# GEMM1 of blocks 3 to 8 of the first layer as seven products over two blocks, with streamed w_out and the second layer's w_in prepared beside it

## The chip, the cores and the metric

The kernel runs on one core of a Trainium2 chip. The metric is the device time of one execution in microseconds (us). Times of single instructions and stretches are read from a trace that the hardware profiler took of one execution. The engines are named as in the profile: PE (TensorE matmul), PEld (its weight loads), DVE (VectorE), ACT (ScalarE), POOL (GpSimd) and SP (SyncE, which issues the DMAs).

## The reference

```python
scores = scale * np.matmul(q_c, k_c.transpose(0, 1, 2, 4, 3))   # chunks of 64 positions
attn = np.exp(scores - np.max(scores, axis=-1, keepdims=True))
attn = attn / (np.sum(attn, axis=-1, keepdims=True) + 1e-09)
out = np.matmul(attn, v_c)
x = out.transpose(0, 2, 1, 3).reshape(4608, 512)
h = x @ w_in;  x = (h * np.cos(h)) @ w_out                       # first layer, w_in 512 x 2048
h = x @ w_in2; y = (h * (1 / (1 + np.exp(-1.702 * h)))) @ w_out2  # second layer
```

All is float32, with 8 x 8 heads, 576 positions and heads of 64.

## The kernel before

The 4608 tokens are nine blocks of 512 (j = 0 to 8), the hidden width 2048 is 16 slices of 128 (f = 0 to 15). Attention runs in 18 pairs of units (two units of 128 tokens), two pairs to a block. A float32 product is three matmuls of a split into a high and a low part (high x high, high x low, low x high), so GEMM1 of one slice and block is 12 matmuls of 128x512, and so is GEMM2.

A plain block has 16 steps. A step is `gemm1` of slice f (into `h`), the cosine chain of the slice on ACT and DVE in turns (ACT L484, DVE L487, ACT L493, ACT L496, DVE L499, then ACT L512 and DVE L515 for the high part `gh` and the low part `gl`), and `gemm2` of slice f - 2 (`LAG`). The first layer's blocks are all plain. While block j runs, attention of block j + 1 is done in it: scores and softmax of its two pairs at steps 0 and 7 (`SJ`), transposes 3 steps and values 5 steps later (`OFFSJ`).

The second layer does block 0 plainly and blocks 1 to 8 in four doubles of two blocks. `pair_of_slices` replaces GEMM1 of two slices on two blocks by seven products of half the depth (42 matmuls where the plain form has 48). The products need left factors (sums and differences of w_in, stored in DRAM as `wc` and loaded for each pair of slices by `load_factors` into `w_xh` and `w_xl`) and right factors (sums and differences of the activations, `right_factor`, kept in the buffers of w_in). The products accumulate in three PSUM tiles, `pb`, `pu` and `pc`. `copied` (L734) copies one to SBUF on ACT, `plus` (L738) adds `pu` to it on DVE, and the next product that accumulates on `pu` must wait until `plus` has read it:

```python
product(0, A11, u, True, False)
c11 = plus(c11)
...
run(6)
product(3, A_S2, u, False, False)
```

`run` puts GEMM2 matmuls of the first of the two blocks between the products (6, 10 and 8). The second block's activations are parked in SBUF. In the second half of a double its 16 GEMM2 steps of 12 matmuls run from the park, split just ahead by `split_park`, and right factors of the next double are made beside them.

The second layer's weights are loaded and converted (L204 to L247, `split_w_parts`) during block 8 of the first layer and block 0 of the second, where the left factors are made and stored as well.

The order on PE is written by hand. On the other engines the framework's scheduler sets it, and each engine then runs its instructions in that order.

Of the kernel before, what the change touches and what calls it, by code (L numbers as in the profile page):

```python
# [19 lines left out]
P = 128  # L20
# [92 lines left out]
def tile_chunk_attention_two_moe(  # L113
# [28 lines left out]
    S0, SJ = (2, 9), (0, 7)  # L142
    OFFS0, OFFSJ = (4, 6), (3, 5)
# [28 lines left out]
    wc = [dr.tile([2, P, 7, 2 * P], F32R, name=f"wc_{i}") for i in range(NP)]  # L172
# [8 lines left out]
    def load_w(dram, layer, which, f):  # L181

        t = wp.tile([P, DM, 2], U32, tag=f"{which}{f}", name=f"raw_{which}{f}")
        nc.sync.dma_start(out=t, in_=dram[f].bitcast(U32).rearrange("p (d w) -> p d w", w=2))
        raw[layer, which, f] = t

    def split_w(layer, which, f):
        for fn in split_w_parts(layer, which, f, layer == 1):
            fn()
        if layer == 1 and which == "i" and f % 2:  # L190
            left_factors(f // 2, T.pop(f - 1), T.pop(f))
# [3 lines left out]
    def split_w_parts(layer, which, f, by_dma=False):  # L195
# [34 lines left out]
        def p5():  # L230
            w = wp.tile([P, 2 * DM], F32R, tag=f"{which}{f}", name=f"{which}{f}")
# [29 lines left out]
    def load_pair(p):  # L261

        if 2 * p >= NU:
            return
        for u in (2 * p, 2 * p + 1):
# [3 lines left out]
        for u in (2 * p, 2 * p + 1):  # L269
# [154 lines left out]

    def att_values(p, tags=("a", "a")):
        for w in range(2):
            att_values_w(p, w, tags)
        for i in range(2):
# [5 lines left out]
    def load_x1(j):  # L434
        if j >= NB:
            return
        for k0 in range(0, KD, 2):
            t = qkp.tile([P, 2, N], F32, tag="qk", name="x1")
            nc.sync.dma_start(out=t, in_=y1[j][k0:k0 + 2].rearrange("k p n -> p k n"))
            xr[j, k0] = t  # L440

# [156 lines left out]
    for j in range(NB - 1):  # L598
        for i in range(PB):
            p = (j + 1) * PB + i  # L600
            s0, offs = (S0[i], OFFS0) if j == 0 else (SJ[i], OFFSJ)
            at((0, j, s0), att_scores, p)
            at((0, j, s0), att_softmax, p)
            at((0, j, s0 + offs[0]), att_transpose, p)
            at((0, j, s0 + offs[1]), att_values, p)
            at((0, j, s0 + offs[1]), load_pair, p + PB)
    at((0, NB - 1, 2), load_x1, 0)
    for k in range(KD):
        at((0, NB - 1, 4 + 2 * k), split_x1, 0, k)
# [8 lines left out]

    A11, A12, A_S1, A_S2, A_S3, A_S4, A22 = range(7)
    PRODUCTS = ("b11", "b21", "t1", "t2", "t3", "b22", "t4")  # L620

    def left_factors(i, t1, t2):
# [5 lines left out]
        for o, x, y, op in (  # L628
            (u[:, :H2], t2[:, :H2], t2[:, H2:], add),
            (u[:, H2:], u[:, :H2], t1[:, :H2], sub),  # L630
            (w[:, :H2], t1[:, :H2], t2[:, :H2], sub),
            (w[:, H2:], t1[:, H2:], u[:, H2:], sub),
        ):
            nc.vector.tensor_tensor(out=o, in0=x, in1=y, op=op)
        hi = ap.tile([P, 2 * DM], F32R, tag="a", name="s_hi")
        lo = ap.tile([P, 2 * DM], F32R, tag="a", name="s_lo")
        for k, src in ((0, u), (1, w)):
            c = slice(k * DM, (k + 1) * DM)
            split(hi[:, c], lo[:, c], src)
        for part, sums in ((0, hi), (1, lo)):  # L640
            first, second = (W[1, "i", 2 * i + k][part] for k in range(2))
            for ops, src in (((0, 2), first), ((2, 6), sums), ((6, 7), second[:, H2:])):
                nc.sync.dma_start(
                    out=wc[i][part, :, ops[0]:ops[1], :].rearrange("p o c -> p (o c)").bitcast(F32),
                    in_=src.bitcast(F32),
                )
# [13 lines left out]
    def right_factor(s, m, k):  # L660

        name = PRODUCTS[m]
        ja, jb = 2 * s + 1, 2 * s + 2
        b11, b12 = xr[jb, 0][:, k], xr[ja, 0][:, k]
        b21, b22 = xr[jb, 2][:, k], xr[ja, 2][:, k]
# [394 lines left out]
```

## Time and profile before

| | us |
|---|---|
| median of 3 runs | 1641.44 (1640.91 to 1643.64) |
| profiled execution, its own time | 1642.49 |
| span of the profiled execution | 1640.7 |
| PE busy | 1604.3 (98%) |
| DVE busy | 879.1 (54%) |
| ACT busy | 844.7 (51%) |

The span runs from the first to the last instruction on the core; 1.8 us of the execution's time lie outside it. The busy shares are means over stages that differ.

### The profile page before, as it was taken

To read this page: it belongs to the slowest core of one execution; us is meant where nothing else is said; L and a number is where in the kernel's file an instruction comes from. 1 tells how busy PE (TensorE), PEld (TensorE's weight loads), DVE (VectorE), ACT (ScalarE), POOL (GpSimd) and SP (SyncE) were. 2 spreads that over 40 slices of the span, in tenths; PEclk is the share of its full clock that TensorE was granted. 3 is DMA by queue.
4 is the path that set the end of the run, shared out by engine and by line. 5 is a ranking of instruction groups with operands and counts; after the bars stand their busy time and mean duration, and the time that the engine had idled before them with its cause. 6 is when DMAs were issued, how large, how long until landed. Compare 5 with 4: busy or idle time off the path is not lost.

```text
span 1640.7 us, 22795 instructions
## 1 busy us (share of the span) xinstructions
PE 1604.3 (98%) x9168; PEld 1321.0 (81%) x9168; DVE 879.1 (54%) x1427; ACT 844.7 (51%) x1419; POOL 57.0 (3%) x69
## 2 busy tenths in 40 slices
PE   5899999999999999999999999999999999999998
PEld 4678888888888888888888788888888888888887
DVE  7796445354445445454688884345434543454442
ACT  6796555455555545555677663343334333333331
POOL 1220000000000000000011110000000000000000
PEclk9899999999999999999999999999999999999999
DMA  9953111011111101110399764340424042404210
GB/s 357 329 117 90 40 44 60 14 66 39 52 40 65 39 16 63 40 52 27 122 282 337 215 186 153 123 163 24 161 115 167 19 170 106 173 14 154 99 68 27
DMA packets 60156, 181.59 MB, mean 111 GB/s; under 512 B 6417, under 2 KB 8465, under 8 KB 60049
## 3 DMA queue, kind: packets, MB, share of 16 engines
q1 hardware_dynamic: 50976, 163.60, 27.4%
q0 software_dynamic: 9072, 16.52, 5.7%
q8 instruction: 72, 1.18, 0.3%
q14 instruction: 36, 0.29, 0.1%
HBM read 130.02 MB, written 33.55 MB: 100 GB/s over the span
## 4 chain that ended last, share of the span: by engine, by line
PE 90%; DVE 3%; DMA 3%; issue 2%; ACT 1%; SPq 0%; POOL 0%; POOLq 0%; ACTq 0%; DVEq 0%
PE y L558 45%; PE h L460 23%; PE pu L723 11%; PE pc L723 5%; PE pb L723 3%; PE x L402 1%; DMA raw_i<-w_in 1%; PE s L295 1%; DMA i<-wt 1%; PE pt_ps L376 1%; DVE wt L218 1%; DMA y<-yo 1%; DVE wt L224 1%; DVE wt L207 0%; ACT wt L204 0%
## 5 line engine op out<-in xcount | busy, mean ns | idle before, releaser
L460 PE MATMUL h<-xh,i 128*128 128x512 f32 x1280 | 426.9, 395 | 15.1 <-DVE r L499 10.5
L558 PE MATMUL y<-o,gh 128*128 128x512 f32 x1152 | 299.8, 389 | 0.6 <-ACT gh L512 0.6
L460 PEld LDWEIGHTS h<-xh,i 128*128 128x128 f32 x1280 | 243.8, 190 | 69.2 <-DVE r L499 12.6
L558 PE MATMUL y<-gh,o 128*128 128x512 f32 x1152 | 295.4, 395 | 0.0
L558 PEld LDWEIGHTS y<-o,gh 128*128 128x128 f32 x1152 | 216.6, 188 | 46.1 <-ACT gh L512 1.0
L460 PE MATMUL h<-xl,i 128*128 128x512 f32 x640 | 252.3, 394 | 0.3 <-DVE xl L423 0.3
L558 PEld LDWEIGHTS y<-gh,o 128*128 128x128 f32 x1152 | 213.1, 188 | 44.6
L487 DVE SCALAR_TENSOR_TENSOR r<-h,r 128x512 f32<-128x512 f32 x144 | 99.4, 690 | 180.3 <-ACT r L484 180.2
L484 ACT ACTIVATE r<-h 128x512 int32<-128x512 f32 x144 | 85.7, 595 | 199.2 <-PE h L460 193.6
L499 DVE SCALAR_TENSOR_TENSOR r<-r,h 128x512 f32<-128x512 f32 x144 | 98.7, 685 | 117.4 <-ACT r L496 117.3
L558 PE MATMUL y<-o,gl 128*128 128x512 f32 x576 | 158.3, 389 | 0.0
L558 PE MATMUL y<-gl,o 128*128 128x512 f32 x576 | 158.3, 389 | 0.0
L460 PEld LDWEIGHTS h<-xl,i 128*128 128x128 f32 x640 | 122.1, 191 | 26.3 <-DVE xl L423 1.0
L515 DVE TENSOR_TENSOR gl<-r,gh 128x512 fp32r<-128x512 f32 x160 | 110.1, 688 | 55.7 <-ACT gh L512 54.9
L512 ACT ACTIVATE gh<-r 128x512 fp32r<-128x512 f32 x160 | 100.5, 628 | 69.5 <-DVE r L499 66.5
L738 DVE TENSOR_TENSOR part<-pu,part 128x512 f32<-128x512 f32 x96 | 66.2, 690 | 129.3 <-ACT part L734 89.2
L558 PEld LDWEIGHTS y<-gl,o 128*128 128x128 f32 x576 | 108.1, 188 | 22.5
L558 PEld LDWEIGHTS y<-o,gl 128*128 128x128 f32 x576 | 108.1, 188 | 22.5
L493 ACT ACTIVATE r<-r 128x512 f32<-128x512 f32 x144 | 91.1, 633 | 60.1 <-DVE r L487 59.8
L734 ACT ACTIVATE part<-pc 128x512 f32<-128x512 f32 x64 | 38.3, 599 | 162.5 <-PE pc L723 162.5
L723 PE MATMUL pu<-x_t,w_xh 128*128 128x512 f32 x384 | 118.2, 389 | 0.0
L700 ACT ACTIVATE r<-part 128x512 f32<-128x512 f32 x96 | 60.4, 629 | 64.7 <-DVE part L738 64.7
(92 smaller groups left out, 1843.9 us busy)
## 6 DMA issues: line engine op xcount, KB each, us to landing
w_xl<-wc SPq DMA_DIRECT2D x32, 896.0 KB, 6.4
w_xh<-wc SPq DMA_DIRECT2D x32, 896.0 KB, 4.6
qk<-qk SPq DMA_DIRECT2D x36, 512.0 KB, 4.4
raw_i<-w_in SPq DMA_DIRECT2D x32, 512.0 KB, 9.2
raw_o<-w_out SPq DMA_DIRECT2D x32, 512.0 KB, 9.2
v<-v SPq DMA_DIRECT2D x36, 256.0 KB, 3.5
y<-yo SPq DMA_DIRECT2D x36, 256.0 KB, 2.3
x<-y SPq DMA_DIRECT2D x18, 512.0 KB, 5.8
```

The costliest lines, as they stand in the source:

```text
L460: nc.tensor.matmul(out=h, lhsT=a[:, w0], rhs=b[:, k, :], start=(k == 0 and i == 0), stop=(k == KD - 1 and i == 2),)
L484: nc.scalar.activation(out=c["r"].bitcast(I32), in_=c["h"], func=AF.Copy, scale=INV_2PI)
L487: nc.vector.scalar_tensor_tensor(out=c["r"], in0=c["h"], scalar=INV_2PI, in1=c["r"].bitcast(I32), op0=ALU.mult, op1=ALU.subtract,)
L493: nc.scalar.activation(out=c["r"], in_=c["r"], func=AF.Sin, scale=math.pi)
L499: nc.vector.scalar_tensor_tensor(out=c["r"], in0=c["r"], scalar=-0.5, in1=c["h"], op0=ALU.add, op1=ALU.mult)
L512: nc.scalar.activation(out=c["gh"], in_=c["r"], func=AF.Copy)
L515: nc.vector.tensor_tensor(out=c["gl"], in0=c["r"], in1=c["gh"].bitcast(F32), op=ALU.subtract)
L558: nc.tensor.matmul(out=ys[d0], lhsT=a, rhs=b, start=(f == 0 and i == 0), stop=(f == NF - 1 and i == 2),)
L700: nc.scalar.activation(out=r, in_=h, func=AF.Sigmoid, scale=1.702)
L723: nc.tensor.matmul(out=out, lhsT=x, rhs=y, start=(start and k == 0 and n == 0), stop=(stop and k == 1 and n == 2), skip_group_check=True,)
L734: nc.scalar.activation(out=t, in_=src, func=AF.Copy)
L738: nc.vector.tensor_tensor(out=t, in0=u, in1=t, op=ALU.add)
```

## The change

Blocks 0 to 2 of the first layer stay plain. Blocks 3 to 8 become three doubles with the same seven products (`by_1024` now serves both layers). For this:

- the first layer's left factors are made in blocks 1 and 2 from the split weights (`left_factors0`) and stored to `wc`; a factor tile has eight parts where it had seven, 1 MB a half where it was 896 KB;
- w_out of the first layer is stored to DRAM in block 1 and streamed back slice by slice (`load_wo`, four buffers), since its buffers now hold the parked activations, the staged attention output and the second layer's new weights;
- attention of blocks 3 and 4 (four pairs) is done in block 2 (`SJ2`), that of blocks 5 to 8 in the second halves of the first two doubles (`SJ3`, four pairs in 11 steps). Its output is staged to SBUF in float32 and turned into right factors (`RIGHT_A`, `RIGHT_B`);
- the second layer's w_in is loaded, converted and made into left factors in the first halves of the three doubles (`prepare1` with stages 0, 1 and 2 in successive pairs of slices, at the slots `PREP`). The third double's second half loads it back (`load_w1`), and w_out of the second layer is converted there and in block 0 of the second layer.

```diff
-    S0, SJ = (2, 9), (0, 7)
-    OFFS0, OFFSJ = (4, 6), (3, 5)
+    S0, OFFS0 = (2, 9), (4, 6)
+    SJ1 = ((0, 3, 5), (7, 10, 12))
+    SJ2 = ((0, 3, 4), (1, 5, 6), (7, 10, 11), (8, 12, 13))
+    SJ3 = ((0, 3, 4), (1, 5, 6), (4, 7, 8), (5, 9, 10))
+    SR = (8, 10)
+    PREP = (0, 3, 5, 8, 11, 13, 16, 19)
...
+    J0 = 3
...
+                    nc.scalar.activation(
+                        out=XS[0, j](2 * b + i)[:, o * P:(o + 2) * P],
+                        in_=xs_t[p][i][:, b].rearrange("p w n -> p (w n)"),
+                        func=AF.Copy,
+                    )
+            return
...
+    for j, p0, starts in ((1, 2 * PB, SJ1), (2, 3 * PB, SJ2)):
+        for p, stages in enumerate(starts, p0):
+            for fn, f in zip((att_begin, att_transpose, att_end), stages):
+                at((0, j, f), fn, p)
...
+    def left_factors0(i):
+        parts = [W[0, "i", 2 * i + k] for k in range(2)]
+        t = []
+        for hi, lo in parts:
+            x = tp.tile([P, DM], F32, tag="t", name="w32")
+            nc.vector.tensor_tensor(out=x, in0=hi.bitcast(F32), in1=lo.bitcast(F32), op=ALU.add)
+            t.append(x)
+        left_factors(0, i, t, parts)
...
+    def store_wo(f):
+        hi, lo = W[0, "o", f]
+        for part, src in ((0, hi), (1, lo)):
+            nc.sync.dma_start(
+                out=wo[f][:, part * DM:(part + 1) * DM].bitcast(F32), in_=src.bitcast(F32)
+            )
+    def load_wo(f):
+        t = wp.tile([P, 2 * DM], F32R, tag=f"o{NF - 4 + f % 4}", name="wo")
+        nc.sync.dma_start(out=t.bitcast(F32), in_=wo[f].bitcast(F32))
+        W[0, "o", f] = t[:, :DM], t[:, DM:]
...
+    def prepare1(i, stage):
+        fs = (2 * i, 2 * i + 1)
+        for k, f in enumerate(fs):
+            if stage == 0:
+                load_w(w2_in, 1, "i", f, tag=f"o{k}")
+            elif stage == 1:
+                for fn in split_w_parts(1, "i", f, False, tag=f"o{2 + k}"):
+                    fn()
+        if stage == 2:
+            left_factors(1, i, [T.pop(f) for f in fs], [W[1, "i", f] for f in fs])
...
-    def load_factors(i):
+    def load_factors(layer, i):
         parts = []
         for part, tag in ((0, "xh"), (1, "xl")):
-            t = xp.tile([P, 7, 2 * P], F32R, tag=tag, name=f"w_{tag}")
-            nc.sync.dma_start(out=t.bitcast(F32), in_=wc[i][part].bitcast(F32))
+            t = xp.tile([P, 8, 2 * P], F32R, tag=tag, name=f"w_{tag}")
+            nc.sync.dma_start(out=t.bitcast(F32), in_=wc[layer][i][part].bitcast(F32))
...
+    RIGHT_A = [(5, k) for k in range(2)]
+    RIGHT_B = [(m, k) for k in range(2) for m in (1, 0, 2, 3, 6, 4)]
...
+    def act_second(layer, j, f, h, keep=None):
         r = tp.tile([P, N], F32, tag="t", name="r")
-        nc.scalar.activation(out=r, in_=h, func=AF.Sigmoid, scale=1.702)
-        nc.vector.tensor_tensor(out=r if keep is None else keep, in0=h, in1=r, op=ALU.mult)
+        dest = r if keep is None else keep
+        if layer == 0:
+            n = r.bitcast(I32)
+            nc.scalar.activation(out=n, in_=h, func=AF.Copy, scale=INV_2PI)
+            nc.vector.scalar_tensor_tensor(
+                out=r, in0=h, scalar=INV_2PI, in1=n, op0=ALU.mult, op1=ALU.subtract
+            )
+            nc.scalar.activation(out=r, in_=r, func=AF.Sin, scale=math.pi)
+            nc.scalar.activation(out=r, in_=r, func=AF.Square)
+            nc.vector.scalar_tensor_tensor(
+                out=dest, in0=r, scalar=-0.5, in1=h, op0=ALU.add, op1=ALU.mult
+            )
+        else:
+            nc.scalar.activation(out=r, in_=h, func=AF.Sigmoid, scale=1.702)
+            nc.vector.tensor_tensor(out=dest, in0=h, in1=r, op=ALU.mult)
...
+    for f in range(NF):
+        at((0, 1, f), store_wo, f)
+    for i in range(NP):
+        at((0, 1 + i // 4, 4 * (i % 4) + 2), left_factors0, i)
+    at((0, J0 - 1, NF - 2), load_factors, 0, 0)
+    for m, k in RIGHT_A:
+        at((0, J0 - 1, 13), right_factor, 0, J0, m, k)
+    for m, k in RIGHT_B:
+        at((0, J0 - 1, 15), right_factor, 0, J0, m, k)
...
+    def by_1024(layer, ja, rest, pair_extra, step_extra, last):
+        jb = ja + 1
+        for i in range(NP):
+            if i + 1 < NP:
+                load_factors(layer, i + 1)
+            if layer == 0:
+                for f in (2 * i, 2 * i + 1):
+                    load_wo(f)
+            for fn, args in pair_extra.get(i, []):
+                fn(*args)
+            pair_of_slices(layer, ja, i, [fn for m in rest for fn in gemm2_list(*m)])
+            if i == 0:
+                flush_y(*rest[-1][:2])
+            rest = [(layer, ja, 2 * i), (layer, ja, 2 * i + 1)]
+        if not last:
+            load_factors(layer, 0)
+        if layer == 0:
+            load_wo(0)
+            load_wo(1)
+        split_park(layer, jb, 0)
+        for m in rest:
+            gemm2(*m)
+        flush_y(layer, ja)
+        for f in range(NF - LAG):
+            if layer == 0:
+                load_wo(f + LAG)
+            split_park(layer, jb, f + 1)
+            for fn, args in step_extra.get(f, []):
+                fn(*args)
+            gemm2(layer, jb, f)
+        split_park(layer, jb, NF - 1)
+        return [(layer, jb, NF - 2), (layer, jb, NF - 1)]
...
+        rest = [(0, J0 - 1, NF - 2), (0, J0 - 1, NF - 1)]
+        slots = [(q, i) for q in range(3) for i in range(NP)]
+        for q in range(3):
+            ja = J0 + 2 * q
+            last = q == 2
+            pair_extra, step_extra = {}, {}
+            for i in range(NP):
+                for stage in range(3):
+                    if slots[PREP[i] + stage][0] == q:
+                        pair_extra.setdefault(slots[PREP[i] + stage][1], []).append(
+                            (prepare1, (i, stage))
+                        )
+            if not last:
+                for p, stages in enumerate(SJ3, (ja + 2) * PB):
+                    for fn, f in zip((att_begin, att_transpose, att_end), stages):
+                        step_extra.setdefault(f, []).append((fn, (p,)))
+                for n, (m, k) in enumerate(RIGHT_A):
+                    step_extra.setdefault(SR[0] + n, []).append((right_factor, (0, ja + 2, m, k)))
+                for n, (m, k) in enumerate(RIGHT_B):
+                    step_extra.setdefault(min(SR[1] + n // 3, NF - LAG - 1), []).append(
+                        (right_factor, (0, ja + 2, m, k))
+                    )
+            else:
+                step_extra[0] = [(load_x1, (0,))]
+                for k in range(KD):
+                    step_extra.setdefault(3 + 3 * k, []).append((split_x1, (0, k)))
+                for f in range(NF):
+                    step_extra.setdefault(f * 2 // 3, []).append((load_w1, (f,)))
+                for f in range(4):
+                    step_extra.setdefault(f, []).append((load_w, (w2_out, 1, "o", f)))
+                    step_extra.setdefault(2 * f + 4, []).append((split_w, (1, "o", f)))
+                for f in range(4, 9):
+                    step_extra.setdefault(2 * (f - 4) + 3, []).append((load_w, (w2_out, 1, "o", f)))
+            rest = by_1024(0, ja, rest, pair_extra, step_extra, last)
```

On DVE, in the first double of the first layer, from the end of its first pair of slices on. L799 is the last step of the cosine chain, L217 to L234 are the conversion of two slices of the second layer's w_in (L207 to L224 before), and L841 is `plus` (L738 before). With the change:

```order
L799 SCALAR_TENSOR_TENSOR park<-r,pu 128x512 [waits Activation_49]
L217 TENSOR_SCALAR wt<-wt 128x512 [waits Activation_49] x2
L222 TENSOR_SCALAR wt<-wt 128x512 [waits DVE_49] x2
L228 SCALAR_TENSOR_TENSOR wt<-raw_i_3622,wt 128x512 [waits DMAHW4_49,DVE_49]
L228 SCALAR_TENSOR_TENSOR wt<-raw_i_3624,wt 128x512 [waits DVE_49]
L234 SCALAR_TENSOR_TENSOR wt<-raw_i_3622,wt 128x512 [waits DVE_49]
L234 SCALAR_TENSOR_TENSOR wt<-raw_i_3624,wt 128x512 [waits DVE_49]
L841 TENSOR_TENSOR part<-pu,part 128x512 [waits PE_49,Activation_49]
```

Eight conversion operations stand between the parking of one pair of slices and the first `plus` of the next. The same place in the second layer, before:

```order
L701 TENSOR_TENSOR park<-pu,r 128x512 [waits Activation_49]
L582 TENSOR_SCALAR yo<-y_8013 128x512 [waits PE_49]
L738 TENSOR_TENSOR part<-pu,part 128x512 [waits PE_49,Activation_49]
L701 TENSOR_TENSOR park<-part,r 128x512 [waits Activation_49]
L738 TENSOR_TENSOR part<-pu,part 128x512 [waits DMASW6_49,Activation_49]
```

There only one output copy stands between them. In the change's other preparations (five of eight) the conversion is spread, and these rows stand between the parking and the first `plus`, with the rest ahead of the parking or behind that `plus`:

```order
L799 SCALAR_TENSOR_TENSOR park<-r,pu 128x512 [waits Activation_49]
L234 SCALAR_TENSOR_TENSOR wt<-raw_i_4037,wt 128x512 [waits DVE_49]
L222 TENSOR_SCALAR wt<-wt 128x512
L841 TENSOR_TENSOR part<-pu,part 128x512 [waits PE_49,Activation_49]
L249 TENSOR_TENSOR i_4166<-wt,i_4166 128x512 [waits DMAHW1_49,DMAHW0_49,Activation_49]
```

On PE, in the second half of the first double of the first layer, step 4: the last values of one pair of attention (L411, into `x`) and the first scores of another (L304, into `s`). `x`, `s` and the transposes' `pt_ps` share a pool of two PSUM tiles. With the change:

```order
L411 MATMUL x_4949<-pt,v 64x64
L411 MATMUL x_4948<-pt,v 64x64
L411 MATMUL x_4949<-pt,v 64x64
L304 MATMUL s_4992<-qk 64x64 [waits DMAHW4_49,PE_49,Activation_49]
L304 MATMUL s_4993<-qk 64x64 [waits PE_49,Activation_49]
```

Scores follow values with nothing between them. Before, values are followed by GEMM2 (L558), and no scores stand in the same step:

```order
L402 MATMUL x_6852<-pt,v 64x64
L402 MATMUL x_6853<-pt,v 64x64
L558 MATMUL y_6384<-gh,o_1119 128x512 [waits Activation_49]
L558 MATMUL y_6384<-gh,o_1119 128x512
L558 MATMUL y_6385<-gh,o_1119 128x512 x2
```

On SP, at the end of block 2: the load of the first double's first left factors, with the stores (L682) of the last left factors ahead of it. `w_xh` takes a buffer that block 2's activations hold.

```order
L682 DMA wc_7_101<-s_part 128x512 [waits DMAHW7_49,Activation_49]
L682 DMA wc_7_101<-s_part 128x512 [waits DMAHW0_49,DVE_49]
L682 DMA wc_7_101<-s_part 128x512 [waits DMAHW1_49,Activation_49]
L682 DMA wc_7_101<-s_part 128x512 [waits DMAHW2_49,DVE_49]
L739 DMA w_xh<-wc_0_94 128x2048 [waits DMAHW3_49,PE_49]
L739 DMA w_xl<-wc_0_94 128x2048 [waits DMAHW4_49]
```

The load waits for PE, which is done with block 2's activations only after the last GEMM1 of that block. In the kernel before no first-layer factors are loaded here.

## Rows read from the trace of the kernel before

**Rows 1.** The page: busy time of each engine, then the chain's share by engine.
```profile
PE 1604.3 (98%) x9168; PEld 1321.0 (81%) x9168; DVE 879.1 (54%) x1427; ACT 844.7 (51%) x1419; POOL 57.0 (3%) x69
...
PE 90%; DVE 3%; DMA 3%; issue 2%; ACT 1%; SPq 0%; POOL 0%; POOLq 0%; ACTq 0%; DVEq 0%
```

**Rows 2.** The chain in block 2 of the first layer: start us, us, what.
```profile
152.07 2.72 PE h L460 x12
154.79 2.72 PE y L558 x12
...
172.00 1.09 PE x L402 x64
```

**Rows 3.** All waits of PE from 150 us to the end: us in total, times, longest.
```profile
PE h L460 <- DVE r L508: 2.2, 2, 1.9
PE y L558 <- ACT gh L512: 0.6, 1, 0.6
```

**Rows 4.** Windows: stretch, its us, busy us of each engine, granted clock, DMA share, GB/s.
```profile
150.69:244.79 94.10, 94.10 (x658) 77.51 (x657) 46.04 (x72) 51.15 (x81) 0.00 (x0) 1.00 0.13 46
...
808.00:902.00 94.00, 94.00 (x416) 77.86 (x415) 79.29 (x145) 73.53 (x127) 14.53 (x16) 1.00 0.97 304
902.00:994.00 92.00, 89.16 (x384) 72.62 (x384) 72.95 (x139) 58.45 (x105) 14.09 (x16) 0.98 0.64 181
979.40:994.37 14.97, 14.97 (x68) 12.40 (x67) 5.96 (x9) 6.08 (x11) 0.00 (x0) 1.00 0.29 78
1097.73:1260.93 163.20, 163.20 (x722) 135.13 (x721) 75.19 (x115) 62.62 (x107) 0.00 (x0) 1.00 0.32 116
```

**Rows 5.** The chain in the second layer's block 0, behind a wait.
```profile
915.70 4.32 PE h L460 x12
920.02 3.02 PE y L558 x12
```

**Rows 6.** Windows around that wait, columns as in rows 4.
```profile
915.00:925.00 10.00, 9.30 (x34) 7.55 (x35) 10.00 (x21) 8.32 (x16) 2.65 (x3) 0.83 0.73 212
```

**Rows 7.** Timeline of a pair of slices in the second layer's first double.
```profile
1031.19 0.60 ACT L734 ACTIVATE part<-pc 128x512 f32<-128x512 f32 x1 [2.96 <-PE pc L723]
...
1031.82 0.69 DVE L738 TENSOR_TENSOR part<-pu,part 128x512 f32<-128x512 f32 x1 [2.87 <-ACT part L734]
...
1033.20 0.62 PE L723 MATMUL pu<-x_t,w_xh 128*128 128x512 f32 x2
```

**Rows 8.** Groups by line and shape: busy us, mean ns of one, idle before.
```profile
L487 DVE SCALAR_TENSOR_TENSOR r<-h,r 128x512 f32<-128x512 f32 x144 | 99.4, 690 | 180.3 <-ACT r L484 180.2
...
L493 ACT ACTIVATE r<-r 128x512 f32<-128x512 f32 x144 | 91.1, 633 | 60.1 <-DVE r L487 59.8
...
L484 ACT ACTIVATE r<-h 128x512 int32<-128x512 f32 x144 | 85.7, 595 | 199.2 <-PE h L460 193.6 <-DMA i<-wt 4.0 <-DMA o<-wt 1.6
...
L207 DVE TENSOR_SCALAR wt<-wt 128x512 f32<-128x512 f32 x64 | 26.9, 432 | 5.1 <-ACT wt L204 5.1
...
L353 DVE TENSOR_TENSOR a<-a,ss 128x1024 f32<-128x1024 f32 x18 | 21.9, 1219 | 0.2
...
L218 DVE SCALAR_TENSOR_TENSOR wt<-raw_i,wt 128x512 uint32<-128x512 uint32 x32 | 21.8, 684 | 0.3
L331 ACT ACT_TABLE_LOAD x17 | 21.8, 1283 | 1.0 <-PEq L1048 0.7
...
L204 ACT ACTIVATE wt<-raw_i 128x512 f32<-128x512 f32 x32 | 21.2, 671 | 9.2 <-DMA y<-yo 4.4 <-DMA i<-wt 4.3 <-DMA raw_i<-w_in 0.5
...
L331 ACT ACTIVATE a<-a 128x1024 f32<-128x1024 f32 x17 | 18.0, 1061 | 7.5 <-DVE a L323 7.3
```

**Rows 9.** The page: DMA issues, KB each, median us to landing.
```profile
w_xl<-wc SPq DMA_DIRECT2D x32, 896.0 KB, 6.4
w_xh<-wc SPq DMA_DIRECT2D x32, 896.0 KB, 4.6
```

More of the change, by code (lines that the diff above doesn't have):

```diff
@@ L636, in left_factors @@
-        lo = ap.tile([P, 2 * DM], F32R, tag="a", name="s_lo")
+        todo = [(A11, parts[0]), (A21, parts[1])]
         for k, src in ((0, u), (1, w)):
[L638 to L642, printed above, removed]
+            if layer == 0:
+                hi, lo = (tp.tile([P, DM], F32R, tag="t", name="s_part") for _ in range(2))
+            else:
+                both = wp.tile([P, 2 * DM], F32R, tag=f"i{NF - 2 + k}", name="s_part")
+                hi, lo = both[:, :DM], both[:, DM:]
+            split(hi, lo, src)
+            todo.append((A_S1 + 2 * k, (hi, lo)))
@@ L643, in left_factors @@
+        for at_op, both in todo:
+            for part in range(2):
                 nc.sync.dma_start(
-                    out=wc[i][part, :, ops[0]:ops[1], :].rearrange("p o c -> p (o c)").bitcast(F32),
-                    in_=src.bitcast(F32),
-                )
+                    out=wc[layer][i][part, :, at_op:at_op + 2, :]
+                    .rearrange("p o c -> p (o c)").bitcast(F32),
+                    in_=both[part].bitcast(F32),
+                )
+    def left_factors0(i):
[6 more added lines that the diff above has]
+        left_factors(0, i, t, parts)
@@ new lines, in store_wo, with load_w1 @@
+    def store_wo(f):
[8 more added lines that the diff above has]
+        W[0, "o", f] = t[:, :DM], t[:, DM:]
+    def load_w1(f):
+        i, k = divmod(f, 2)
+        t = wp.tile([P, 2 * DM], F32R, tag=f"i{f}", name="w1")
+        op = A21 if k else A11
+        for part in range(2):
+            nc.sync.dma_start(
+                out=t[:, part * DM:(part + 1) * DM].bitcast(F32),
+                in_=wc[1][i][part, :, op:op + 2, :].rearrange("p o c -> p (o c)").bitcast(F32),
+            )
+        W[1, "i", f] = t[:, :DM], t[:, DM:]
@@ L756, in pair_of_slices @@
         c12 = plus(c12)
-        act_second(ja, f1, c12)
+        act_second(layer, ja, f1, c12)
         run(10)
@@ L1015, in tile_chunk_attention_two_moe @@
+        for ja in range(1, NB, 2):
+            last = ja + 2 == NB
+            step_extra = {}
+            if not last:
+                step_extra[0] = [(load_x1, (ja + 2,)), (load_x1, (ja + 3,))]
+                for n, (m, k) in enumerate(RIGHT):
+                    step_extra.setdefault(4 + n // 2, []).append((right_factor, (1, ja + 2, m, k)))
+            rest = by_1024(1, ja, rest, {}, step_extra, last)
         for m in rest:
```

165 lines of the change are left out of this document (77 added, 88 removed).

## The prediction

> **What bounds the kernel now.** The page comes first: PE is busy 1604.3 us of the span, and 90% of the chain that ended last is PE's [rows 1]. The chain shows how dense that is: in a plain block, twelve 128x512 matmuls take 2.72 us, so 0.2267 us each, and groups follow each other without a gap [rows 2]. The list of PE's waits from 150 us on, that is for all but the opening and the first block, has 2.8 us in all, of which 2.2 lie in the second layer's block 0 [rows 3]. The windows then tell the stages apart: a plain block with attention takes 94.10 us with DVE at 46.0 and ACT at 51.2, and PE is busy all of it; a pair of slices of a double takes 14.97 us, which is 66 matmuls of 0.2267, with DVE at 5.96 [rows 4]. So a removed matmul is worth its 0.2267 us, as long as nothing new makes PE wait. PE waits nowhere in the stretch that is rebuilt, so every new wait there is a loss.
>
> My base is the profiled execution's own 1642.49 us; the median of the runs is 1.05 us lower, and I take that off at the end.
>
> **What it removes.** Three doubles of eight pairs of slices need 42 in place of 48 matmuls: 3 x 8 x 6 = 144, times 0.2267 = **-32.6**. That the products run at this rate when nothing holds them, the 14.97 us show.
>
> **The second layer's start.** Before, block 8 carries the whole conversion (DVE 79.3 of 94.0 us, PE still full) and block 0 the rest of it: in its window PE is idle 2.84 us and the granted clock is 0.98 [rows 4]. The idle time is paid and the clock costs 2% of 92, so 1.8. With the change that window keeps 12 slices of w_out and the right factors, with no conversion of w_in; by count DVE has there 32 steps of activations, 14 right factors and 8 subtractions at 0.69 and 12 conversions of 2.2, near 64 us of 87, under the 79.3 of 94 that hid. I take **-4.6**, bounds -4.7 and -2.
>
> **The entry to the first double.** The first factors can load only after block 2's last GEMM1, since they take its buffers, and only GEMM2 of one slice (2.72 us) is left to cover them. The two 896 KB halves land after 4.6 and 6.4 us [rows 9]; by 8/7 for the larger tiles, 5.3 and 7.3. The second one late is 7.3 - 2.7 = 4.6. After a wait PE comes back slowly: behind the 1.9 us wait of [rows 3], twelve matmuls took 4.32 us instead of 2.72 [rows 5], in a window whose granted clock is 0.83, between the two levels of 1.2 and 2.4 GHz [rows 6]. That is 1.6 more. With the issue behind four stores I take **+7**; bounds 5 (no clock loss) and 12 (the halves one after the other, 5.3 + 7.3 - 2.7, with the clock).
>
> **Attention in the second halves.** The step there has GEMM2 alone, 2.72 us, where a plain step has 5.44. So the three steps between scores and transposes shrink from 16.3 us to 8.2, plus 1.1 for another pair's scores [rows 2], 9.3 in all. The softmax needs: four operations on 128x512 of 0.68 (2.7), the part of the exponentials that is not beside them (1.2 of 2 x 1.06), the sum and the normalisation (1.22 each), small ones 0.4, and between them in queue order three `gl` on DVE (0.69 each) and two `gh` on ACT (0.63 each): 10.1 to 10.3 with the hops between engines [rows 8]. The table load of 1.28 us is issued ahead and lies beside the maximum. The first transposes come 1.0 late. Next, scores stand right behind values: both PSUM tiles must first be emptied by staging copies, of which two, and the `gh` ahead of them, precede the first score: about 1.5. Scores behind transposes wait for two copies of 0.6 and the hops with a `gh` between: 1.7. Values one step behind transposes: 0.4. That is 4.6 for a half and **+9.2** for two. What a wait of 1 to 1.7 us does to the clock no row shows; between nothing and 1.6 for each of six, I take **+2**. Together, bounds 5 and 16. The right factors of the next double are made in the last steps and are done before their first product; DVE has room there (16 split steps of 0.69).
>
> **The preparation in the first halves.** Here the wait is on `plus`. A product needs its PSUM tile `pu` read by `plus`. In the second layer the copy at 1031.19 is followed by `plus` at 1031.82, done at 1032.51, and PE's next product starts at 1033.20: 0.7 us of slack [rows 7]. That is the cover into which the conversion goes.
>
> Time from a pair's last product: the cosine chain that ends in the parking is 0.60 + 0.69 + 0.63 + 0.63 + 0.69 and hops, 3.35 us. In the next pair 24 matmuls (5.44 us) pass before PE needs the first `plus`. In the three preparations in the second pair of slices of a double (stage 1), eight conversion operations stand between the parking and that `plus`. At their spacing back to back they take 0.43 + 3 x 0.35 + 0.69 + 3 x 0.61 = 4.0 (alone they are 0.43 and 0.68 [rows 8]). So `plus` ends at 3.35 + 4.0 + 0.69 = 8.0; ACT's two copies of the raw weights (0.67 each) fall among the chain's ACT steps and delay it by some 0.6: 8.6, a wait of **3.2**. The clock goes with it, as behind the 1.9 us wait: 1.6 more. The pair after (sums and differences of stage 2) loses 0.3. Three times 5.1 is **+15.3**.
>
> In the other five preparations two operations stand there (0.96 in sequence), and three more ahead of the parking push the chain back; `plus` ends near 6.1 instead of 5.44, which is 0.7, and stage 2 in the pair after, with six operations of 3.0 us on DVE, costs 0.9. Five times 1.6 is **+8**. The sum is +23.3. Lower bound 8: the three waits without ACT's delay (2.6) and without the clock, the five hidden. Upper bound 28: each of the eight as long as the three are, less the clock.
>
> **Small things.** Stores in block 1, left factors in blocks 1 and 2 (plain blocks, which hid 79 us of DVE), reloading of w_in in the last second half: hidden by PE-bound steps, 0 to 6, I take **+1.5**.
>
> **Sum.** -32.6 - 4.6 + 7 + 9.2 + 2 + 23.3 + 1.5 = +5.8, so 1648.3 for a profiled execution and 1647 for the median.
>
> **The rivals.**
>
> *Faster, PE hardly waits for `plus`.* The place is the first `plus` of a pair of slices, the price 23.3 us. For faster by 0.2% (3.3 us, about what a measurement of this kernel can tell from no change) the new waits together must stay below 33.9; with 19.7 for the others, preparation must stay below 14. The point is there when the clock keeps its level after the three waits (4.8 less) and the five spread ones cost half (4 less). For it: ACT and DVE are at 5.4 to 6 us of 15 in such a pair before, so they catch up at once, and one window is thin evidence on the clock. Against it: a fixed order on each engine, in which the rows stand as they do. With preparation at 8 to 12 and second halves at 5 to 9 the time is 1624 to 1637, centre 1630.
>
> *No change.* The same waits, without the clock's part (some 8 us in three terms): 1639 to 1645.
>
> *Slower, DMA.* In the three first halves each pair of slices loads factors of 2.1 MB and w_out of 1.05 MB; preparation adds 1.05 of raw weights, and 2.1 of stores two pairs later. Two of the eight storing pairs carry 6.3 MB, six 5.25 MB, in 15 us. Before, the densest stage with full PE moved 304 GB/s at a DMA share of 0.97 [rows 4]. At that rate 5.25 MB take 17.3 us and 6.3 MB 20.7: 6 x 2.3 + 2 x 5.7 = 25 us, less what the pairs with 3.15 MB (10.4 us) catch up, for one pair of factors is loaded ahead. With half of it the time is 1660, with all 1673. Against it: the mean over the 24 pairs is 281 GB/s, below 304, and that stage of before was full of small packets.
> The Trainium skill, "DMA: Bandwidth & Descriptors" (Specifications), gives about 358 GB/s as the limit of HBM for a core; by that estimate only the two pairs of 6.3 MB would be late, by 2.6 us each, and this rival would end at 1652. The 304 of this trace stays under that figure, so it does not refute it.
>
> **How the numbers follow.** Forecast (waits as summed, 1642 to 1656) 0.50, of which a fifth falls within 0.2%; faster 0.33; no change 0.05; DMA 0.12. Slower by over 0.2% is 0.8 x 0.50 + 0.12 less a little of the forecast's lower edge, 0.50; within, 0.16; faster, 0.34. The range reaches down over most of the faster case, to 1627, and up over half of the DMA case, to 1663.
>
> **What would show it.** The rows of `pu` products should show PE idle near 3 us behind `plus` in the second pair of slices of each of the three doubles, and under 1 us in the others; a wait near 5 us on `w_xl` at the entry; waits of 1 to 1.7 us of scores and transposes on ACT and DVE in two second halves; the second layer's block 0 without a wait. I am wrong if PE is idle under 12 us in the three first halves together, or if waits on `w_xl` or `wo` are large inside them.

## The result and the profile after

The changed kernel takes 1654.24 us (median of 4 runs, 1652.68 to 1655.79) against 1642.01 us for the kernel before beside it: a ratio of 1.0074, 95% interval 1.0056 to 1.0091. It is slower by 12 us. The profiled execution took 1655.18 us, 12.7 more than that of before.

The page after, part 1 and the chain by engine:

```profile
PE 1584.1 (96%) x9024; PEld 1296.7 (78%) x9024; DVE 985.2 (60%) x1621; ACT 889.6 (54%) x1545; POOL 42.3 (3%) x53
...
PE 78%; DVE 8%; DMA 6%; ACT 5%; issue 3%; SPq 0%; POOL 0%; DVEq 0%; POOLq 0%; ACTq 0%
```

Against [rows 1]: PE has exactly 144 matmuls less, but only 20 us less busy time where 144 at 0.2267 are 32.6: the matmuls behind waits ran slower. Its part of the chain fell from 90 to 78%; DVE, DMA and ACT took that over. All waits of PE from 150 us on (us in total, times, longest), which were 2.8 us before [rows 3]:

```profile
PE pu L826 <- DVE part L841: 16.5, 16, 3.2
PE pb L826 <- DMA w_xh<-wc: 5.8, 1, 5.8
PE y L593 <- DMA wo<-wo: 3.8, 4, 1.0
PE s L304 <- ACT xs L456: 2.0, 4, 0.8
PE pb L826 <- DMA w_xl<-wc: 1.2, 1, 1.2
PE s L304 <- ACT pt L392: 1.0, 4, 0.4
PE x L411 <- DVE a L332: 0.3, 2, 0.2
```

That is 30.6 us of four kinds: on `plus`, on the first factors, on w_out and in attention. The largest, on `plus`, has three waits of 3.17 and thirteen of 0.26 to 0.75. The timeline of DVE shows the first of the three (start, us, instruction):

```profile
370.44 0.69 DVE L799 SCALAR_TENSOR_TENSOR park<-r,pu 128x512 f32<-128x512 f32 x1
371.04 0.94 DVE L217 TENSOR_SCALAR wt<-wt 128x512 f32<-128x512 f32 x2
371.90 0.75 DVE L222 TENSOR_SCALAR wt<-wt 128x512 uint32<-128x512 uint32 x2
372.57 1.28 DVE L228 SCALAR_TENSOR_TENSOR wt<-raw_i,wt 128x512 uint32<-128x512 uint32 x2
373.77 1.28 DVE L234 SCALAR_TENSOR_TENSOR wt<-raw_i,wt 128x512 uint32<-128x512 uint32 x2
374.98 0.68 DVE L841 TENSOR_TENSOR part<-pu,part 128x512 f32<-128x512 f32 x1
```

The eight conversion operations stand in one block between the parking (L799) and `plus` (L841); DVE does not idle, and PE starts its next product at 375.72. The chain at the entry to the first double (start, us, what) shows the other loss:

```profile
340.75 9.06 DMA w_xl<-wc
...
349.85 2.07 PE pb L826 x4
351.93 2.56 PE pu L826 x6
354.49 1.72 PE pc L826 x6
356.21 1.38 PE y L593 x6
```

The load was issued 1.8 us after the buffer came free, behind stores that waited for DVE, and took 9.06 us; behind the wait six matmuls take 2.56 us and not 1.36. Windows of stretches (columns as in rows 4):

```profile
95.00:140.00 45.00, 37.89 (x207) 30.44 (x208) 36.89 (x70) 35.45 (x62) 9.40 (x12) 0.89 1.07 320
...
541.21:728.92 187.71, 180.19 (x1265) 146.12 (x1264) 137.29 (x227) 124.92 (x218) 0.00 (x0) 1.00 0.77 269
870.00:900.00 30.00, 26.15 (x111) 20.09 (x110) 7.23 (x11) 7.33 (x13) 1.72 (x2) 1.00 1.05 360
903.38:990.42 87.04, 87.04 (x385) 72.07 (x384) 59.53 (x104) 47.03 (x84) 10.45 (x12) 1.00 0.45 124
```

The first row is a surprise: late in block 0, DMA is full. The same stretch in the kernel before:

```profile
95.00:140.00 45.00, 42.17 (x298) 33.81 (x298) 40.20 (x76) 39.84 (x70) 10.55 (x12) 0.96 0.54 109
```

320 GB/s in place of 109, and PE 4.3 us less busy. The second row is the middle double: 187.71 us, where its 720 matmuls (163.2) and four pairs of attention (3.5 each) need 177.3. The third is the last second half, in which w_out comes late. The fourth is the second layer's block 0, which now runs without a gap; before, from its first matmul at 885.49 to the first product at 977.89, it took 92.4.

### The profile page after: what moved, and what is told of

Read it like the earlier page. It is cut to its first block, busy times and chain, and to the rows that moved or that the text cites. A ratio compares the mean times of both kernels' runs of the same rounds, so it can differ in the third digit from the quotient of the medians.

```text
span 1653.4 us, 23446 instructions
## 1 busy us (share of the span) xinstructions
PE 1584.1 (96%) x9024; PEld 1296.7 (78%) x9024; DVE 985.2 (60%) x1621; ACT 889.6 (54%) x1545; POOL 42.3 (3%) x53
## 4 chain that ended last, share of the span: by engine, by line
PE 78%; DVE 8%; DMA 6%; ACT 5%; issue 3%; SPq 0%; POOL 0%; DVEq 0%; POOLq 0%; ACTq 0%
PE y L593 41%; PE pu L826 15%; PE h L495 9%; PE pc L826 7%; PE pb L826 3%; DMA raw_i<-w_in 2%; DVE part L841 1%; ACT r L797 1%; DVE r L794 1%; PE x L411 1%; DMA wo<-wo 1%; DMA i<-wt 1%; ACT r L798 1%; ACT r L793 1%; PE pt_ps L385 1%
## 5 line engine op out<-in xcount | busy, mean ns | idle before, releaser
L826 PE MATMUL pu<-x_t,w_xh 128*128 128x512 f32 x672 | 209.8, 394 | 16.5 <-DVE part L841 16.5
L841 DVE TENSOR_TENSOR part<-pu,part 128x512 f32<-128x512 f32 x168 | 115.8, 689 | 161.1 <-ACT part L837 105.9
L593 PE MATMUL y<-gh,wo 128*128 128x512 f32 x768 | 203.2, 393 | 3.8 <-DMA wo<-wo 3.8
L593 PEld LDWEIGHTS y<-gh,wo 128*128 128x128 f32 x768 | 142.2, 188 | 35.5 <-issue 5.4
L826 PEld LDWEIGHTS pu<-x_t,w_xh 128*128 128x128 f32 x672 | 125.1, 188 | 48.8 <-DVE part L841 23.2
L495 PE MATMUL h<-xh,i 128*128 128x512 f32 x384 | 131.4, 404 | 16.4 <-DVE r L534 11.2
L826 PE MATMUL pu<-x_t,w_xl 128*128 128x512 f32 x336 | 131.3, 391 | 0.0
L593 PE MATMUL y<-gl,wo 128*128 128x512 f32 x384 | 105.6, 389 | 0.0
L495 PEld LDWEIGHTS h<-xh,i 128*128 128x128 f32 x384 | 74.8, 195 | 34.4 <-DVE r L534 12.7
L593 PE MATMUL y<-gh,o 128*128 128x512 f32 x384 | 101.7, 403 | 0.0
L593 PEld LDWEIGHTS y<-gh,o 128*128 128x128 f32 x384 | 71.8, 192 | 15.4
```

The costliest lines, as they stand in the source:

```text
L495: nc.tensor.matmul(out=h, lhsT=a[:, w0], rhs=b[:, k, :], start=(k == 0 and i == 0), stop=(k == KD - 1 and i == 2),)
L593: nc.tensor.matmul(out=ys[d0], lhsT=a, rhs=b, start=(f == 0 and i == 0), stop=(f == NF - 1 and i == 2),)
L826: nc.tensor.matmul(out=out, lhsT=x, rhs=y, start=(start and k == 0 and n == 0), stop=(stop and k == 1 and n == 2), skip_group_check=True,)
L841: nc.vector.tensor_tensor(out=t, in0=u, in1=t, op=ALU.add)
```

## The experiments

Medians in us; "plus", "wo" and "entry" are PE's waits on `plus`, on streamed w_out, and at the start of the first double (on `w_xh`, `w_xl` and in two runs `x_t`, or on `plus` where no load was late). All ratios are to the kernel before, run beside each (1641.7 to 1642.4). The intervals are some 2.5 us to each side: those of e2 and e3 overlap with that of the change, so their gains of 3.6 and 3.5 us rest as much on the waits in their traces as on the times.

| run | median | ratio, 95% interval | plus | wo | entry |
|---|---|---|---|---|---|
| the change | 1654.24 | 1.0074 (1.0056 to 1.0091) | 16.5 | 3.8 | 7.0 |
| e1 preparation from the middle | 1648.05 | 1.0034 (1.0021 to 1.0047) | 8.4 | 8.4 | 6.0 |
| e2 first factors early | 1650.60 | 1.0051 (1.0034 to 1.0068) | 14.1 | 4.3 | 4.3 |
| e3 reloading spread | 1650.73 | 1.0055 (1.0040 to 1.0070) | 16.2 | 1.3 | 6.7 |
| e4 stores held back | 1648.70 | 1.0039 (1.0024 to 1.0054) | 16.3 | 4.3 | 7.5 |
| e5 conversion split | 1643.10 | 1.0009 (0.9999 to 1.0018) | 6.8 | 6.3 | 6.9 |
| e6 and late factors | 1643.36 | 1.0007 (0.9997 to 1.0016) | 8.6 | 5.4 | 6.8 |
| e7 all together | 1627.54 | 0.9909 (0.9894 to 0.9924) | 6.7 | 2.5 | 0 |
| e8 before with stores | 1649.31 | 1.0036 (1.0022 to 1.0049) | | | |
| e9 left factors in block 1 | 1630.68 | 0.9932 (0.9917 to 0.9947) | 6.9 | 3.2 | 3.6 |
| e10 spread further | 1622.53 | 0.9882 (0.9865 to 0.9898) | 0 | 3.0 | 3.6 |
| e11 right factors deferred | 1613.83 | 0.9827 (0.9812 to 0.9842) | 0 | 2.2 | 1.2 |
| e12 spread alone | 1635.19 | 0.9953 (0.9939 to 0.9967) | 1.0 | 5.0 | 6.9 |

**e1.** Stages 1 and 2 are issued inside a pair of slices:

```diff
         act_second(layer, ja, f2, c22)
+        for fn, args in mid:
+            fn(*args)
         run(8)
```

> The changed kernel with the conversion and the sums of the second layer's w_in issued from the middle of a pair of slices (behind the third plus), so that on DVE no conversion stands between a pair's parking and the next pair's first plus. Theory (plus is late because the conversion stands ahead of it in DVE's order): the 16.5 us of PE waits on plus fall under 2, their slow restarts (some 6 us) go too, and the time is 1631 to 1635, about 21 us under the changed kernel's 1654.2. Rival (the first halves are held by DMA, which moves 325 GB/s there): the waits move to w_xh, w_xl or wo and the time stays above 1645.

6 us less, not 21. The pair that had waited 3.17 us was freed, but single conversion operations now stood ahead of the first `plus` of the pair behind it. The timeline of DVE in e1, where PE waited until 387.20:

```profile
385.86 0.69 DVE L234 SCALAR_TENSOR_TENSOR wt<-raw_i,wt 128x512 uint32<-128x512 uint32 x1
386.46 0.69 DVE L841 TENSOR_TENSOR part<-pu,part 128x512 f32<-128x512 f32 x1
```

Eight pairs of slices, one for each preparation, still lost 1.4 us each (1.05 of wait), and waits on `wo` grew from 3.8 to 8.4 us: both theories were partly right.

**e2.** The first factors in w_out's buffers:

```diff
-    at((0, J0 - 1, NF - 2), load_factors, 0, 0)
+    at((0, J0 - 1, 9), load_first_factors)
...
-    PREP = (0, 3, 5, 8, 11, 13, 16, 19)
+    PREP = (1, 3, 5, 8, 11, 13, 16, 19)
```

> The changed kernel with the first double's first left factors loaded into the buffers of w_out's slices 0 to 3 from step 9 of block 2 on (and the first preparation one pair of slices later, since it uses the same buffers). Theory (the load can start only behind block 2's last GEMM1 and behind four stores on SP): the waits of 5.8 and 1.2 us on w_xh and w_xl go, and with them the slow matmuls behind; 7 to 10 us less, 1644 to 1647. Rival (the right factors on DVE are as late as the load, so the wait only changes its name): PE waits 4 us or more on x_b or x_t at the same place and the time is above 1650.

The rival, in its milder form: 3.6 us less, and a wait of 4.3 us on the first `plus` in place of 7.0 on the load, since right factors keep DVE busy until then (e11 shows it). A by-product: in the first double, where the preparation now starts one pair later, the 3.17 us wait is gone (0.75 at most); the other two doubles keep theirs. So those three waits belong to the place behind a double's first pair. The output copies of the block before stand there too; no run shows whether they are the reason.

**e3.** The reloading spread:

```diff
-                    step_extra.setdefault(f * 2 // 3, []).append((load_w1, (f,)))
+                    step_extra.setdefault(min(f, NF - LAG - 1), []).append((load_w1, (f,)))
```

> The changed kernel with the reloading of the second layer's w_in in the last second half spread over one slice a step instead of three slices in two steps. Theory (the four waits on wo, 3.8 us with 1.4 of slow restarts, come from transfers that share the stretch at 360 GB/s): they fall under 1 us and the time is 1649 to 1651. Rival (wo is late because it is issued behind instructions of SP that wait for something else): the waits stay and the time is 1653 to 1655.

As the theory had it, but for two waits that stay, 1.3 us in all.

**e4.** The stores held back:

```diff
+    def gate(out, n):
+        src = GF[max(GF)][0]
+        nc.sync.dma_start(out=out.bitcast(F32), in_=src[0:1, 0:n].bitcast(F32))
...
     def store_wo(f):
         hi, lo = W[0, "o", f]
+        gate(wo[f][0:1, 0:2 * DM:DM], 2)
...
     def left_factors0(i):
+        gate(wc[0][i][:, 0, 0:8:A21, 0], 4)
```

> The changed kernel with each store of w_out and of w_in's parts made to wait for a tiny transfer from an activation of block 1 (24 transfers of 8 or 16 bytes), so that no store runs while block 0 still converts its weights. Theory (the stores crowd the transfers of the conversion in block 0): DMA in 95 to 140 us falls from 316 to near 110 GB/s, the waits at 108 and 127 us go back to those of before (none, 2.8) and the time is 1647 to 1649. Rival (the opening varies from run to run, the stores cost nothing): 1653 to 1656.

The theory holds: no wait at 108 us, 2.8 us at 122 us, and 0.6 on DVE's `r` besides. The same window of e4:

```profile
95.00:140.00 45.00, 41.58 (x291) 33.14 (x283) 40.33 (x76) 39.42 (x69) 10.53 (x12) 1.00 0.53 106
```

**e8** is the mirror: the kernel before, plus the stores.

```diff
+    for f in range(NF):
+        for which in "oi":
+            at((0, 1, f), store_spare, which, f)
```

> The kernel before with nothing but the 16.8 MB of stores added: both parts of w_out and w_in of the first layer written to DRAM from block 1's steps, as the change does, and never read. Theory (the stores crowd the conversion's transfers in block 0): a wait near 2.8 us on i, 4.3 in place of 2.8 us for the transposes, and 1647 to 1650, 5 to 7 us slower than before. Rival (the changed kernel's opening was unlucky): no change, 1641 to 1643.

7.0 us slower. Its waits of PE between 95 and 150 us, where the kernel before has only 2.8 on `a`:

```profile
PE pt_ps L376 <- DVE a L353: 4.5, 1, 4.5
PE h L460 <- DMA i<-wt: 3.3, 2, 2.8
PE h L460 <- DVE r L499: 0.4, 1, 0.4
```

**e5** issues the conversion of one slice behind the first activation of a pair of slices, that of the other behind the second, and the sums behind the first activation of the next pair. **e6** also loads the next double's first factors from step 8 of a second half.

```diff
+                    mid[0].append((convert1, (args[0], 0)))
+                    mid[1].append((convert1, (args[0], 1)))
...
-            load_factors(layer, 0)
+            step_extra.setdefault(8, []).append((load_factors, (layer, 0)))
```

> The changed kernel with the two slices' conversion issued apart, one behind the first and one behind the second activation of a pair of slices, the sums behind the first; the rows of DVE then have at most one conversion operation just ahead of any plus. Theory (the conversion's place in DVE's order makes plus late): PE's waits on plus fall from 16.5 us to under 2 in total, and each of the eight pairs that took 16.3 us with the preparation issued from the middle takes 15.0. Second theory, on what is given back: first halves that run faster leave less time for the same bytes, so the waits on wo at the start of the second halves stay at 8 us or grow; the time is then 1643 to 1646. Rival (those wo waits came from the moved stores): wo waits fall to the 3.8 us of the changed kernel and the time is 1634 to 1638.

> As the kernel with the split preparation, and the next double's first left factors (2.1 MB) loaded from step 8 of a second half on instead of at its start. Theory (w_out's slices at the start of a second half are queued behind these 2.1 MB and the attention's loads): the wo waits of the first two second halves (about 3 us and their slow restarts) fall under 0.5 us, those of the third stay; 3 to 6 us less than the kernel with the split preparation. Rival (the stretch as a whole has too many bytes): the waits only move to later steps, and the time is the same.

e5 came out at the time of the second theory, but not by its cause: waits on `wo` fell from the 8.4 us of e1 to 6.3, and 6.8 us were left on `plus` where I had expected under 2, since the second slice's conversion now stood ahead of the third `plus` (e10 moves it away). In e6 my premise failed: of e5's waits on `wo` only 0.5 us, not 3, lay in the first two second halves. That wait went, and 1.3 us of new waits on `plus` came in the second pairs of the next two doubles; the time is the same.

**e7** has e6, e3, e2 and e4 together, with block 2's attention in 11 steps.

> All of it together: split preparation, late first factors, the reloading spread, the first double's factors and right factors early (attention of block 2 in 11 steps in place of 14), and the stores held back to block 1. If the four losses of the changed kernel are separate and add (22.9 + 10.3 + 5.3 + 6.5 us by its trace), and DMA does not take them back: 1609 to 1620, faster than before by 1.4 to 2%. If DMA is what bounds the first halves once plus is in time: 1625 to 1640, with waits on w_xh, w_xl or wo.

Faster than before, and short of the sum of the four. The time lies in the range I gave for a bound by DMA, but without the waits that go with it: none on `w_xh` or `w_xl`, 2.5 us on `wo`, and 6.7 still on `plus`. Block 2 paid for the tight attention; its waits of PE from 230 to 345 us:

```profile
PE s L304 <- ACT xs L456: 2.8, 1, 2.8
PE s L304 <- ACT pt L392: 0.5, 2, 0.3
```

**e9** goes back to 14 steps and makes all left factors in block 1; **e10** also moves the second slice's conversion.

```diff
-        at((0, 1 + i // 4, 4 * (i % 4) + 2), left_factors0, i)
+        at((0, 1, 2 * i + 1), left_factors0, i)
...
-                    mid[1].append((convert1, (args[0], 1)))
+                    mid[2].append((convert1, (args[0], 1)))
```

> The kernel with all of it together, except that block 2's attention keeps the change's 14 steps and right factors their steps 13 and 15, and all eight pairs of left factors are made in block 1 (four of them stood in block 2). Theory (the tight attention cost block 2 a wait of 2.8 us for ACT's staging copies and the slow matmuls behind it, some 5 us; DVE is late for the first plus of the double, 4.3 us where only the load was early, because left and right factors meet at the end of block 2): no wait of scores in block 2, at most 1.5 us at the entry, 1621 to 1625. Rival (right factors alone keep DVE busy to the end of block 2): a wait of 3 to 4 us on plus at the entry, 1626 to 1629.

> The same kernel with the second slice's conversion issued behind the third plus of a pair of slices instead of the second. Theory (the 0.7 to 1.25 us that are left on plus, with 0.3 of slow restart, come from one conversion operation ahead of the third plus): they fall under 0.3 us each, and the time is 6 to 9 us under the kernel whose second conversion stands behind the second plus. Rival (the first halves are then held by their bytes): waits on wo, w_xh or w_xl of the same size instead, and the same time.

In e9 my theory fell, and at 1630.68 the time is above the rival's range too: 3.6 us on `plus` at the entry stayed, and 2.1 us on block 0's output copies came in block 1, where all left factors are made now. In e10 the theory held: of the waits on `plus` only the one at the entry is left.

**e11** keeps the spread, puts the left factors back and defers four right factors; **e12** is the change with the spread conversion alone.

```diff
+            if layer == 0 and ja == J0 and i == 0:
+                mid[0].extend((right_factor, (0, J0, m, k)) for m in (4, 6) for k in range(2))
```

> The spread kernel with left factors in blocks 1 and 2 as the change has them, and four of the first double's fourteen right factors (those of the fifth and the seventh product, which are used last) made behind the first plus of the double instead of ahead of it. Theory (the first plus, 3.6 us late at the entry, waits only because all right factors stand ahead of it on DVE, eight operations of 0.69 more than it needs): the wait falls under 0.5 us, the waits in block 1 on the output copies go too, and the time is 1613 to 1618. Rival (the last attention values are too late for the first right factors): a wait of 2 us or more on x_b, x_t or plus stays, 1619 to 1622.

> The changed kernel with the conversion spread alone (first slice behind the first activation of a pair of slices, second slice behind the third plus, sums behind the first activation of the next), all else as in the change. It measures what the preparation's place costs: theory, the 16.5 us of waits on plus are gone and every pair of slices but the first takes 15.0 us, 12 to 16 us less in the three first halves beyond the 1643.1 of the kernel with the second slice behind the second plus, or rather, since half of the waits went there already, 1634 to 1638, with 3 to 8 us of waits on wo given back. Rival (bytes bound the first halves): pairs of slices stay at 15.5 us or more with waits on w_xh or w_xl, 1640 or above.

e11 is the best version, 1.7% under the kernel before. The wait at the entry fell from 3.6 to 1.2 us, not under 0.5, and the waits in block 1 went. All its waits of PE from 150 us on:

```profile
PE y L593 <- DMA wo<-wo: 2.2, 1, 2.2
PE s L304 <- ACT xs L456: 2.0, 4, 0.8
PE pu L857 <- DVE part L872: 1.2, 1, 1.2
PE s L304 <- ACT pt L392: 1.1, 4, 0.4
PE x L411 <- DVE a L332: 0.4, 2, 0.2
```

e12 is 19.0 us under the change. Its waits from 330 to 860 us, which are the three first halves, two second halves and the start of the third, where the wait on `wo` lies:

```profile
PE pb L830 <- DMA w_xh<-wc: 5.7, 1, 5.7
PE s L304 <- ACT xs L456: 2.0, 4, 0.8
PE y L593 <- DMA wo<-wo: 1.2, 1, 1.2
PE pb L830 <- DMA w_xl<-wc: 1.2, 1, 1.2
PE s L304 <- ACT pt L392: 1.1, 4, 0.4
PE pu L830 <- DVE part L845: 1.0, 2, 0.7
PE x L411 <- DVE a L332: 0.4, 2, 0.2
```

Behind the entry no wait on a factor is left in the first halves: their bytes are not what bounds them.

## Why the prediction was right, and where it was not

It forecast slower, at an even chance, 1647 us in 1627 to 1663; 1654 was measured. So the direction was right and the loss, 12 us, was over twice the 5 that I forecast. Its terms against the trace after, which has 12.7 us more than that of before:

| term | forecast | trace after | read from |
|---|---|---|---|
| 144 matmuls | -32.6 | -32.6 | 9024 for 9168, at 0.2267 |
| second layer's block 0 | -4.6 | -5.4 | 87.04 for 92.40 |
| entry | +7 | +10.3 | 5.78 idle, first pair 19.51 for 14.96 |
| second halves | +11.2 | +5.4 | 2 x 2.7 over matmuls and attention |
| preparation | +23.3 | +22.9 | all other pairs of the first halves over 14.96 each |
| small things | +1.5 | +11.8 | opening 6.5 (block 2's first scores at 243.13 for 236.62), w_out late in the last second half 5.3 |
| sum | +5.8 | +12.4 | |

**Preparation** was right in its mechanism, its place and its size, and the runs confirm it: three waits of 3.17 where 3.2 stood, thirteen small ones, and 19.0 us less in e12, which moves nothing else. That is under 22.9, since in e12 these pairs still stand 2.1 us over 14.96 and PE waits 1.2 us more on `wo`. One part of it went another way: I charged 1.6 us of slow matmuls behind each of the three waits; only the first paid it, and the sum came out because every short wait also cost some 0.3 of restart. That was luck: in e2, e3 and e4 the same wait had slow matmuls of up to 2.9 us behind it (last section).

**The step that failed** is the one on small things: "Stores in block 1, left factors in blocks 1 and 2 [...] hidden by PE-bound steps", at 1.5 us where 11.8 were lost. I took the stores' time from the step at which the code issues them. On SP they stand behind the loads of the weights and ahead of block 0's output, and wait only for their data, so they run as soon as a weight is converted, in block 0: in the trace after, the first is issued at 71.4 us and the first output of block 0 at 157.2. There each conversion ends in a transfer that POOL issues (`i<-wt`, `o<-wt`). Issues between 95 and 140 us (count, KB each, median us to landing), first before, then with the change:

```profile
o<-wt POOLq DMA_DIRECT2D x7, 256.0 KB, 3.3
...
wc<-i SPq DMA_DIRECT2D x21, 256.0 KB, 6.2
wo<-o SPq DMA_DIRECT2D x20, 256.0 KB, 7.5
o<-wt POOLq DMA_DIRECT2D x7, 256.0 KB, 7.0
```

In e4 these transfers land after 3.3 us again, in e8 after 7.1 to 7.8. PE then waits for a weight (2.8 us at 108), and its wait on `a` grows from 2.8 to 4.3; how the stores reach that second wait no trace shows, but it comes and goes with them. e4 takes the stores away from there and gains 5.5 us; e8 puts them into the kernel before and loses 7.0. I had read SP's order at the entry only. The same step called the reloading of w_in in the last second half hidden; there it meets w_out's raw weights and the stream of w_out at 360 GB/s, and PE waits 3.8 us on `wo`. e3 spreads it, which takes these waits to 1.3.

**Second halves** were over-estimated, 11.2 for 5.4. The first transposes were hardly late (no wait of `pt_ps` is in the list after 150 us), so my softmax chain of 10.1 to 10.3 us was too long: in the second double it takes 9.5, from the end of the scores at 675.29 to 684.75, against a cover of 9.3. Scores behind values waited 1.0 and scores behind transposes 0.5, where I had 1.5 and 1.7. This error and the one before have opposite signs and hid each other in part.

**The entry** had the right place, but the load took 9.06 us where I scaled 7.3 from the median (most of the wait, 5.8 us, is on `w_xh`, the rest on `w_xl`), and the slow matmuls behind it cost some 3.3 and not 1.6. The second part of it I did not see: behind the load stands DVE. e2 takes the load away and 4.3 us on `plus` appear; e9 keeps 3.6 of them; e11 lets four right factors pass behind the first `plus`, and 1.2 is left.

**The second layer's start** came out near its size, though I had read its rows from the wrong stretch. Block 0 of the second layer runs from 885.49 to 977.89 in the kernel before, with DVE at 82.2 of 92.4 us, and block 8 of the first layer from 791.39 to 885.49, with DVE at 75.2 of 94.1; my windows began 16.5 us later. PE's idle time (2.84) and the clock (0.98) are the same in both readings, so the term held.

**The DMA rival** had the right traffic in the wrong place. By the Trainium skill, "DMA: Bandwidth & Descriptors" (Specifications), some 358 GB/s is the limit from HBM to a core. In e12 a window of 30 us moved 402, nearly all of it loads from HBM, so with one core at work that figure was no ceiling here:

```profile
860.00:890.00 30.00, 26.26 (x112) 20.49 (x112) 7.27 (x12) 7.91 (x12) 0.00 (x0) 1.00 1.04 402
```

In the first halves DMA moved 280 to 304 GB/s (change, e11, e12), and behind the entry no run has a wait on a factor. Small packets were no argument either: packets under 512 B are 11% in the 304 GB/s stage of before and 11% in this window of e12. What did come late was w_out, at the start of second halves and in the last one: 8.4 us in e1, 6.3 in e5, 5.0 in e12, there all in the last.

**The faster rival** had the right point of decision. With preparation at 2 us, e12 is at 1635, in that rival's 1624 to 1637. The agreement is in part luck: that range has preparation at 8 to 12 and small things at 1.5, and in e12 the stores in block 0 and the late w_out, which made up the 11.8, are still there.

Open is what the rest of the waits cost in e11 (2.2 us on `wo`, 3.5 in the second halves); no run was made for them.

## What to carry to other kernels

DVE was idle for 40% of the span and still delayed PE by 3.2 us at a time, when eight short operations stood in its order ahead of the one that was awaited: look for what the busy engine waits for, and at the rows ahead of it, not at the share of busy time. Issuing the same work from other places in the program, in smaller groups, was worth 19 us here and nothing else had to change. Small groups alone were not enough: e1 and e5 spread it too and kept waits of 0.7 to 1.25 us, and it was the place, by how much slack each `plus` has, that decided. A store with no reader nearby ran here as soon as its data and its queue allowed, in block 0 and not in block 1 where the code has it: place it by what it will collide with, and give it a dependency if it must come later.

## What the runs showed of the hardware that was not expected

The same wait did not always slow PE. Behind a wait of 3.17 or 3.18 us on `plus`, at the same place of the program, the granted clock of the next 6 us was 1.00 in four cases and 0.50 to 0.74 in seven (11 such waits in the change, e2, e3 and e4). Windows of the change, from the end of its first and its second such wait:

```profile
375.72:381.72 6.00, 6.00 (x20) 4.87 (x21) 3.22 (x5) 2.59 (x6) 0.00 (x0) 0.73 0.84 332
564.94:570.94 6.00, 6.00 (x26) 4.99 (x27) 3.73 (x6) 3.28 (x7) 0.00 (x0) 1.00 0.88 310
```

And of e3, at its first and its third:

```profile
373.77:379.77 6.00, 6.00 (x14) 4.74 (x15) 2.53 (x4) 2.37 (x5) 0.00 (x0) 0.50 0.91 363
...
753.62:759.62 6.00, 6.00 (x26) 4.99 (x27) 3.73 (x6) 3.26 (x7) 0.00 (x0) 1.00 0.75 288
```

At 0.50 PE runs at the lower of its two levels, 1.2 and 2.4 GHz, for all of the 6 us. The pair of slices with the wait takes 18.4 us where the clock stays at 1.00, 19.9 to 20.0 at 0.72 to 0.74, and 21.0 to 21.3 at 0.50 to 0.53. Against 14.96 us without a wait, a wait of this length so cost between 3.5 and 6.3 us, and one execution does not tell which.
